# The third and fourth column block of the last gate's weights as two transfers, of 72 and of 56 rows

## Chip, cores and metric

The kernel runs on one core of one Trainium2 chip. The metric is the device time of one execution in microseconds (us), the median of several runs.

## The reference

The reference is one decode step of a transformer block with adaptive layer norm, for four sequences (B = 4) of one token, D = 512. Everything is in float32.

```
mod = silu(c) @ w_mod                 # c: 4 x 512, w_mod: 512 x 3072 -> six vectors of 512
sa, ca, ga, sb, cb, gb = mod
h = layernorm(x) * (1 + ca) + sa
x = x + ga * attention(h, k_cache, v_cache, wq, wo)   # 32 query heads, 8 key heads, last 2048 positions
h = layernorm(x) * (1 + cb) + sb
out = x + gb * ((silu(h @ w1) * (h @ w3)) @ w2)       # w1, w3: 512 x 1792, w2: 1792 x 512
```

The change concerns the weights of gb, the last of the six: gb = silu(c) @ w_mod[:, 2560:], a product of 4 x 512 with 512 x 512.

## The kernel before

The kernel is written for the engines directly: each engine has its own stream of instructions, and waits on semaphores by hand. The host lays every weight out so that a load is a plain copy of 128 rows, one for each SBUF partition. A load of rows of n columns is 128 x 4n bytes.

Three large buffers take the data: KV[0], KV[1] (64 KB in each of 128 partitions) and WP (32 KB). Attention runs over eight key heads, one after the other in KV[0] and KV[1]; WP holds the projections' weights for a pair of heads. After that the same buffers take the rest: KV[0] the modulation weights wm_in and the first feed-forward weights f1_in, KV[1] the rest of them (f2_in, two loads), the gate's weights gb_in, and then w2_in in six pieces of 4, 4, 2, 2, 1 and 1 blocks of 512 columns (W2_CUTS).

All large loads but one (t1_in, and the four rows of x, on ACT's queue) are issued by SP, in the order of the code, by `load(dst, src, sem)` (L89), which adds 16 to a semaphore once the transfer has landed. Before a buffer is filled anew, SP waits for the matmuls that read it. For KV[1]'s last contents that is L120, `S.wait_ge(o_done, G)`: the attention's last product. Behind it SP issues nine loads: f2_in twice, gb_in, w2_in six times (L121 to L125). Then it waits for the end to store the output.

gb_in holds w_mod's last 512 columns with 512 input rows laid out as four column blocks of 512 for each partition: partition p holds in block k the 512 weights of input row 128k + p. In KV[1] they lie in columns 6144 to 8191. Their one reader is the loop at L444 on TensorE: four matmuls, each with one block as its moving operand and 4 columns of sc (silu of c, transposed) as its weights. The results go to four groups of rows of the PSUM bank bM; ScalarE copies them to gb_sb (L448), and a later set of matmuls adds the four groups and turns them to the output's layout (L464).

The order of TensorE's work at the end: up and gate products from f1_in and f2_in, transposes of them (L437), `T.wait_ge(dgb, 16)` and gb's four matmuls, then for each piece of w2 a wait for its landing (L453) and its matmuls; between the pieces the sum of gb (after the first) and that of the first eight blocks of w2 (after the third). After the last piece come two operations of VectorE (L478, L480) and the store.

Of the kernel before, what the change touches and what calls it, by code (L numbers as in the profile page):

```python
# [43 lines left out]
def block_kernel(nc, x_in, t0_in, t1_in, kv_in, w_in, wm_in, f1_in, f2_in, gb_in, w2_in, out):  # L44
    T, v, s, gp, S = nc.tensor, nc.vector, nc.scalar, nc.gpsimd, nc.sync

    def sems(names):
        return [nc.alloc_semaphore(n) for n in names.split()]

    def sb(name, cols, rows=P):  # L50
        return nc.alloc_sbuf_tensor(name, (rows, cols), F32).ap()
# [8 lines left out]
    dx, dt0, dt1, dkv, dk, dva, dvb, dwo, dm, df1, df2a, df2b, dgb = sems("dx dt0 dt1 dkv dk dva dvb dwo dm df1 df2a df2b dgb")  # L60
# [5 lines left out]
    KV = [sb("KV0", 16384), sb("KV1", 16384)]  # L66
# [21 lines left out]
    def load(dst, src, sem):  # L88
        S.dma_start(dst, src).then_inc(sem, 16)  # L89
# [30 lines left out]
    S.wait_ge(o_done, G)  # L120
    load(KV[1][:, :3072], f2_in[:, :3072], df2a)  # L121
    load(KV[1][:, 3072:6144], f2_in[:, 3072:], df2b)
    load(KV[1][:, 6144:8192], gb_in, dgb)
    for a, b, sem in zip(W2_CUTS[:-1], W2_CUTS[1:], dw):
        load(KV[1][:, 8192 + a * 512 : 8192 + b * 512], w2_in[:, a * 512 : b * 512], sem)  # L125

# [313 lines left out]
    t_hid = V.op(v.tensor_mul(view(hidT)[:, :, :3], view(sT)[:, :, :3], view(bS)[:, :, :3, :B]))  # L440


    T.wait_ge(dgb, 16)
    for k in range(4):  # L444
        ins = mm(bM[32 * k : 32 * k + B, :], sc[:, k * B : (k + 1) * B], KV[1][:, 6144 + 512 * k : 6144 + 512 * (k + 1)])
    ins.then_inc(pe, 1)
# [85 lines left out]
```

## Time and profile before

| | |
|---|---|
| median of 3 runs | 242.96 us (242.74 to 242.99) |
| the profiled execution | 243.09 us, span 241.7 us |
| busy: PE, PEld, DVE, ACT, POOL | 137.8, 38.0, 38.6, 25.1, 1.7 us |
| granted TensorE clock, mean | 0.843 |
| bytes moved | 101.34 MB, 419 GB/s over the span |
| gb_in: bytes, issue to landing | 1024 KB, 22.8 us |

PE is TensorE's matmuls, PEld its weight loads, DVE is VectorE, ACT ScalarE, POOL GpSimd, SP the engine that issues the loads; PEq and SPq are the sequencers of PE and SP. The span runs from the first to the last instruction, and times in the trace count from its start. The 16 DMA engines of the core share each large transfer. A row "A <-B" names what is written and what is read; in the chain of work that ended last, each row has its start, its length and what ran then.

### The profile page before, as it was taken

The page shows a single profiled execution, that of the slowest core. Times are in us where ns is not written, and L with a number is a line of the kernel's source. Part 1 is how long each engine was busy: PE and PEld are TensorE (multiplying, and loading weights), DVE is VectorE, ACT ScalarE, POOL GpSimd, SP SyncE. Part 2 cuts the span into 40 slices and gives each one's busy share as a digit, 9 for nine tenths or more (in the row PEclk, how much of TensorE's full clock was granted, in tenths as well). Part 3 has the DMA queues.
Part 4 walks back from the last instruction along what each step waited for, and adds up shares of the span by engine and source line. Part 5 has one row for each costly group of instructions (what it writes and reads, how often), then busy time and mean ns, then how long its engine had stood idle before and what let it go on. Part 6 is the DMA issues. An engine that isn't in the chain of part 4 may idle for free. (4 is left out here: it accounts for less than half of the span.)

```text
span 241.7 us, 2238 instructions
## 1 busy us (share of the span) xinstructions
PE 137.8 (57%) x940; PEld 38.0 (16%) x940; DVE 38.6 (16%) x126; ACT 25.1 (10%) x54; POOL 1.7 (1%) x14
## 2 busy tenths in 40 slices
PE   3004677726771478267713782877137869656964
PEld 0000122201220013112200130121001312111211
DVE  3003203202200022022000220130002222133112
ACT  2002002100010011010100110011002100133110
POOL 2000000000000000000000000000000000000000
PEclk9999959968798579887985898679758997995999
DMA  7998989899989898999898989998989999999993
GB/s 266 440 511 358 510 361 499 369 423 439 504 369 499 369 499 370 423 428 504 369 499 369 499 369 423 434 510 369 499 347 445 442 396 445 449 431 394 413 415 116
DMA packets 4045, 101.34 MB, mean 419 GB/s; under 512 B 452, under 2 KB 580, under 8 KB 1096
## 3 DMA queue, kind: packets, MB, share of 16 engines
q1 hardware_dynamic: 3888, 99.17, 95.7%
q10 hardware_dynamic: 152, 2.11, 2.1%
q8 instruction: 3, 0.05, 0.1%
q14 instruction: 2, 0.02, 0.0%
HBM read 101.20 MB, written 0.07 MB: 419 GB/s over the span
## 5 line engine op out<-in xcount | busy, mean ns | idle before, releaser
L266 PE MATMUL bS<-KV,Z 128*16 128x512 f32 x256 | 42.7, 828 | 39.2 <-PEq L269 39.2
L266 PE MATMUL bO<-KV,pT 128*16 128x512 f32 x256 | 32.5, 652 | 0.5
L266 PEld LDWEIGHTS bS<-KV,Z 128*16 128x16 f32 x256 | 9.3, 123 | 67.1 <-issue 67.1
L222 DVE TENSOR_REDUCE MX<-bS 128x1 f32<-128x512 f32 x8 | 5.5, 692 | 80.4 <-PE bS L266 80.4
L266 PE MATMUL bM<-KV,sc 128*4 128x512 f32 x24 | 6.9, 801 | 16.6 <-DVE sc L188 16.6
L230 ACT ACTIVATE p_sb<-bS,NB 128x512 f32<-128x512 f32 x8 | 5.5, 687 | 101.2 <-DVE NB L228 101.2
L287 PE MATMUL bP<-ident,p_sb 128*128 128x128 f32 x32 | 5.6, 303 | 16.6 <-PEq L269 16.6
L266 PE MATMUL bA<-WP,oT 128*4 128x512 f32 x64 | 11.1, 773 | 4.3 <-PEq L269 4.3
L266 PEld LDWEIGHTS bO<-KV,pT 128*16 128x16 f32 x256 | 8.2, 107 | 23.9 <-issue 23.9
L251 ACT ACTIVATE o_sb<-bO,LB 128x512 f32<-128x512 f32 x8 | 5.5, 687 | 48.8 <-PE bO L266 48.8
L266 PE MATMUL bQ<-WP,hT 128*4 128x512 f32 x64 | 9.2, 647 | 0.6 <-DVE hT L197 0.6
L287 PE MATMUL bX<-ident,o_sb 128*128 128x128 f32 x32 | 5.0, 280 | 7.2 <-PEq L269 7.2
L254 DVE TENSOR_REDUCE oT<-bX 128x16 f32<-128x64 f32 x8 | 1.8, 224 | 43.6 <-PE bX L287 43.6
L287 PEld LDWEIGHTS bP<-ident,p_sb 128*128 128x128 f32 x32 | 3.6, 148 | 24.0 <-issue 24.0
L287 PE MATMUL bT<-ident,q_sb 128*128 128x128 f32 x32 | 5.5, 298 | 3.2 <-PEq L269 3.2
L201 ACT ACTIVATE q_sb<-bQ 128x512 f32<-128x512 f32 x8 | 4.7, 593 | 13.3 <-PE bQ L266 13.3
L287 PEld LDWEIGHTS bX<-ident,o_sb 128*128 128x128 f32 x32 | 3.4, 141 | 14.3 <-issue 14.3
L235 DVE COPY pT<-bP 128x256 f32<-128x256 f32 x8 | 3.4, 424 | 13.5 <-PE bP L287 13.5
L266 PE MATMUL bQ<-KV,h2T 128*4 128x512 f32 x32 | 5.3, 816 | 0.3 <-DVE h2T L398 0.3
L287 PEld LDWEIGHTS bT<-ident,q_sb 128*128 128x128 f32 x32 | 3.6, 150 | 8.0 <-issue 7.7
L266 PEld LDWEIGHTS bM<-KV,sc 128*4 128x4 f32 x24 | 1.0, 104 | 22.4 <-DVE sc L188 18.2
L266 PE MATMUL bX<-KV,sc 128*4 128x512 f32 x24 | 4.2, 592 | 0.0
(100 smaller groups left out, 65.2 us busy)
## 6 DMA issues: line engine op xcount, KB each, us to landing
WP<-w_in SPq DMA_DIRECT2D x3, 4096.0 KB, 22.0
KV<-kv_in SPq DMA_DIRECT2D x1, 4096.0 KB, 24.3
KV<-f_in SPq DMA_DIRECT2D x1, 4096.0 KB, 28.0
KV<-kv_in SPq DMA_DIRECT2D x1, 3072.0 KB, 31.1
KV<-wm_in SPq DMA_DIRECT2D x1, 3072.0 KB, 18.4
KV<-f_in SPq DMA_DIRECT2D x2, 1536.0 KB, 19.2
KV<-t_in SPq DMA_DIRECT2D x1, 2056.0 KB, 12.2
WP<-t_in ACTq DMA_DIRECT2D x1, 2048.0 KB, 12.4
```

What stands on the lines that cost most here:

```text
L201: A.op(s.mul(q_sb, bQ, DH**-0.5), q_ok)
L222: t = V.op(v.reduce_max(MX[:, 0:1], bS, axis=AX.X))
L230: A.op(s.activation(p_sb, bS, AF.Exp, bias=NB[:, 0:1], accum_out=SM[:, 0:1]), p_ok)
L235: v.tensor_copy(pT.rearrange("p (t b c r) -> p c b t r", t=NT, b=B, c=4), bP.rearrange("p (c b i) -> p c b i", c=4, b=B)[:, :, :, :16].rea ...
L251: A.op(s.mul(o_sb, bO, LB[:, 0:1]), o_ok)
L254: V.op(v.tensor_reduce(oT.rearrange("p (r b) -> p r b", r=R), diag, axis=AX.X, op=ALU.add), ot_ok)
L266: return T.matmul(o, lhsT, rhs, start=start, stop=stop, skip_group_check=True)
L287: ins = T.transpose(dst[:, c * P : (c + 1) * P], src[:, c * P : (c + 1) * P], ident)
```

## The change

gb_in comes as three transfers in place of one. The first has columns 0 to 1023 of all 128 rows, the first two blocks, 4 KB for each row. The second has the other two blocks for rows 0 to 71, the third for rows 72 to 127. All three add to the same semaphore, dgb, and TensorE waits for 48 instead of 16. The bytes, their places and their order in the queue, behind f2_in and ahead of w2_in, stay as they were.

```diff
@@ -120,7 +120,9 @@
     S.wait_ge(o_done, G)
     load(KV[1][:, :3072], f2_in[:, :3072], df2a)
     load(KV[1][:, 3072:6144], f2_in[:, 3072:], df2b)
-    load(KV[1][:, 6144:8192], gb_in, dgb)
+    load(KV[1][:, 6144:7168], gb_in[:, :1024], dgb)
+    for rows in (slice(0, 72), slice(72, 128)):
+        load(KV[1][rows, 7168:8192], gb_in[rows, 1024:], dgb)
     for a, b, sem in zip(W2_CUTS[:-1], W2_CUTS[1:], dw):
         load(KV[1][:, 8192 + a * 512 : 8192 + b * 512], w2_in[:, a * 512 : b * 512], sem)
@@ -440,7 +442,7 @@
-    T.wait_ge(dgb, 16)
+    T.wait_ge(dgb, 48)
     for k in range(4):
         ins = mm(bM[32 * k : 32 * k + B, :], sc[:, k * B : (k + 1) * B], KV[1][:, 6144 + 512 * k : 6144 + 512 * (k + 1)])
     ins.then_inc(pe, 1)
```

## The prediction

> **What bounds the kernel now.** I read the page's head and its slices of time, then the chain that ended last, the end of the timeline, and last the DMA engines' share in short windows of the end. The profiled execution took 243.09 us, its span 241.7; the median of the runs is 242.96, 0.13 us less, so a difference worked out on the trace is put on the median as it is. About 0.2%, 0.49 us, is what a measurement of this kernel can tell from no change.
>
> ```profile
> span 241.7 us, 2238 instructions
> DMA  7998989899989898999898989998989999999993
> DMA packets 4045, 101.34 MB, mean 419 GB/s; under 512 B 452, under 2 KB 580, under 8 KB 1096
> q1 hardware_dynamic: 3888, 99.17, 95.7%
> q10 hardware_dynamic: 152, 2.11, 2.1%
> DMA 12%; PE 3%; SPq 1%; DVE 0%; issue 0%
> KV<-gb_in SPq DMA_DIRECT2D x1, 1024.0 KB, 22.8
> ...
> 209.62 0.04 issue
> 209.67 0.43 SPq L89
> 210.10 0.04 issue
> 210.14 28.79 DMA KV<-w_in
> 238.93 0.04 issue
> 238.97 0.45 PE bX L266 x8
> 239.42 0.02 issue
> 239.44 0.30 DVE yt L478
> ```
>
> The 16 DMA engines are busy in nearly every slice, and the chain ends with the last piece of w2: issued by 210.14, landed at 238.93. From there to the end stand 2.7 us that nothing here touches. So the kernel ends when the slowest of the 16 engines has written its part of the last piece. Sixteen engines at 419 GB/s give 26.2 GB/s each: 4 KB in 0.156 us, 8 KB in 0.313 us.
>
> The packet counts tell how a transfer is dealt out. SP's queue has 27 transfers of 128 rows, and 3888 = 27 x (128 + 16): a packet for each row and one closing write for each engine. ACT's queue has one of 128 rows and x's four rows: 152 = (128 + 16) + (4 + 4). So four rows ran on four engines, 128 rows on sixteen.
>
> The next view is the end in windows: after the times, PE, PEld, DVE, ACT and POOL, the clock, the DMA engines' share and GB/s.
>
> ```profile
> 110.00:120.00 10.00, 7.53 (x52) 1.93 (x56) 1.18 (x6) 0.69 (x1) 0.00 (x0) 0.83 0.97 419
> ...
> 228.40:230.20 1.80, 1.79 (x12) 0.20 (x7) 1.13 (x4) 0.22 (x1) 0.00 (x0) 1.00 0.99 414
> 230.40:232.60 2.20, 1.52 (x12) 0.47 (x12) 0.74 (x2) 0.02 (x1) 0.00 (x0) 1.00 1.03 428
> 232.80:235.00 2.20, 1.23 (x16) 0.29 (x16) 0.00 (x0) 0.63 (x2) 0.00 (x0) 1.00 0.98 397
> ...
> 236.60:237.00 0.40, 0.40 (x16) 0.17 (x8) 0.37 (x1) 0.00 (x0) 0.00 (x0) 1.00 1.01 348
> 237.00:237.40 0.40, 0.40 (x12) 0.11 (x8) 0.00 (x0) 0.00 (x0) 0.00 (x0) 1.00 0.33 123
> 237.40:237.80 0.40, 0.11 (x8) 0.09 (x8) 0.00 (x0) 0.00 (x0) 0.00 (x0) 1.00 0.20 77
> 237.80:238.20 0.40, 0.40 (x16) 0.23 (x13) 0.00 (x0) 0.00 (x0) 0.00 (x0) 1.00 0.13 51
> 238.20:238.60 0.40, 0.37 (x16) 0.11 (x8) 0.00 (x0) 0.00 (x0) 0.00 (x0) 1.00 0.06 20
> 238.60:239.00 0.40, 0.19 (x12) 0.03 (x8) 0.00 (x0) 0.00 (x0) 0.00 (x0) 1.00 0.00 0
> ```
>
> Share times 16 is the number of engines still at work: 16 until 237.0, then 5.3, 3.2, 2.1, 1.0 in steps of 0.4 us, and none after 238.6. So about twelve engines end near 237.1, and four late ones near 237.5, 237.9, 238.2 and 238.5. The last is 1.4 us behind the twelve. The view doesn't number the engines.
>
> **The change, part by part.**
>
> Bytes for each engine. Now gb_in is 128 rows of 8 KB, eight rows or 64 KB an engine. Then 128 half rows of 4 KB come first, eight or 32 KB an engine. The 72 and the 56 rows that follow don't divide by 16. The packet counts fit "as many engines as divide the rows, at most 16", and by that 72 rows run on 12 engines with six rows each, and 56 on 14 with four each. Twelve engines then carry 8 + 6 + 4 = 18 rows of 4 KB, 72 KB, 8 KB more than now: 0.31 us. Two carry 48 KB, 16 KB less: -0.63 us. Two carry 32 KB, 32 KB less: -1.25 us. Shorter rows also cost: between the windows 230.4 to 232.6 (rows of 8 KB) and 232.8 to 235.0 (8 and 4 KB) the rate falls from 428 to 397 GB/s, so at most 8% of the 2.4 us that 64 KB take, 0.2 us, and at least nothing; I take 0.1. The twelve are 0.4 us later, two 0.5 earlier, two 1.2 earlier. If 72 rows ran on 16 engines after all, with four or five rows each, every engine would be within 4 KB, 0.16 us, of now. [...]
>
> Where the rows go. Every large transfer now spreads over 128 partitions, so at any time sixteen engines write to all of them. The trace can't tell whether 26.2 GB/s is the limit of an engine or of the eight partitions that it writes. The new ones go to partitions 0 to 71 and then 72 to 127, one half after the other, by 12 and 14 engines. The price has two ends. If the limit is the engine's, nothing is added to the sum above. If it is that of eight partitions, the first half takes at most 8 x 26.2 = 210 GB/s. 64 of the 72 rows go there, 256 KB, in 1.25 us, where six rows an engine would need 0.94. The 56 rows then all go to the other half, 224 KB in 1.07 us, where four rows an engine would need 0.62. Together 2.3 us instead of the 1.25 that the second 4 KB of all rows take now: an engine that carries both is 1.1 us later. A late engine fares worse. When it writes its ten rows, the early ones are at w2 already, and w2 goes to all partitions; with half of the rate its ten rows take 3.1 instead of 1.25 us, 1.9 later.
>
> The nearest rows are 419 GB/s in the window from 110 to 120 us, where the rows are 16 KB and longer, and 414 to 428 where they are 8 KB, all partitions in use. A limit that stays the same over such different rows doesn't come from the engines' work on each row, which leaves the width of the path between engine and partitions; of that path one end is as likely as the other to be the narrow one, and if both are equally wide, the partitions' end decides as soon as two engines meet there. So I take the crowding as the likelier, with both ends kept. [...] No row of this trace shows a large transfer to half of the partitions.
>
> Issues. SP issues two more transfers ahead of w2's six, 0.43 + 0.04 us each, so w2's are issued 0.94 us later. That costs nothing while the engines' queues are full. gb_in takes 22.8 us from issue to landing, nearly all of it behind earlier transfers, and this backlog covers the 0.94; without it the end would move by that much. SP has nothing else to do until the output.
>
> The wait. PE now waits for three landings of gb_in instead of one. Behind that wait on PE stand gb's matmuls and all of w2's; ACT waits for their result.
>
> ```profile
> 207.29 0.43 SPq L89 DMA_DIRECT2D KV<-gb_in  x1
> ...
> 230.99 0.55 PE L437 MATMUL bS<-ident,u_sb 96*128 96x96 f32 x4 [0.80 <-DVE u_sb L434]
> 231.47 1.04 PE L266 MATMUL bM<-KV,sc 128*4 128x512 f32 x8
> 232.58 0.59 ACT L448 COPY gb_sb<-bM 128x512 f32<-128x512 f32 x1 [3.95 <-PE bM L266]
> 232.77 1.04 PE L266 MATMUL bO<-KV,hidT 128*4 128x512 f32 x8 [0.26 <-DMA KV<-w_in]
> 235.16 1.04 PE L266 MATMUL bO<-KV,hidT 128*4 128x512 f32 x8 [1.14 <-DMA KV<-w_in]
> 237.71 1.05 PE L266 MATMUL bX<-KV,hidT 128*4 128x128 f32 x24 [0.29 <-DMA KV<-w_in]
> ```
>
> PE starts them at 231.47 without a wait. gb_in was issued at 207.29 and took 22.8 us, so it landed at 230.1, 1.4 us before. A delay up to 1.4 us is hidden there. With 1.9 us PE would start 0.5 later and finish at 233.0, where w2's first piece, later by as much, keeps it waiting until about 234.4 anyway. PE waits for w2 in each of the later rows, so it follows the DMA to the end, and what the last landing moves, the end moves.
>
> The sum with crowding. The twelve go from 237.1 to 238.2, below the 238.5 of now. A late engine that is one of the twelve decides: the third, 238.2 + 1.9 = 240.1, is 1.6 us after 238.5; the second, 237.9 + 1.9, 1.3; the last itself, 1.9. I take the middle, 1.6: 242.96 + 1.6 = 244.5 us.
>
> **The rivals.**
>
> Balance pays (faster). No crowding, and the four late engines are the four that are relieved. Then the late ones end at 238.5 - 1.2 = 237.3, the twelve at 237.1 + 0.4 = 237.5, and the end comes 1.0 us earlier, with 0.1 left for the spread of the twelve 0.9: 242.1. The amounts speak for it: 1.2 and 0.5 us is about what the late ones are behind by. Against it: nothing ties the late ones to the last four; it decides only if every late engine is among them. If just one that ends at 238.2 is not, it ends at 238.6 and the gain is gone.
>
> Balance that misses (no change). No crowding, and one or more of the late engines are among the twelve: the second late one gives 237.9 + 0.4 = 238.3, 0.2 us gained; the third 0.1 lost; the last 0.4 lost. So 242.8 to 243.4, within 0.2%. For it: four of sixteen engines are late, and only four are relieved. Against it: only the crowding. The same holds when 72 rows run on all 16 engines, at 0.16 us either way.
>
> Crowding with the late engines relieved. Then the twelve end last, at 238.2 and up to 0.6 later where two share a place with w2: 0.3 earlier to 0.3 later, no change that can be told.
>
> **How the numbers follow.** Crowding with a late engine among the twelve: 0.60, 244.5, its own range 243.9 to 245.9 (from 0.9 to 2.9: a late engine that meets two others at a place has a third of the rate for part of its rows, 1.0 more). Balance that misses and crowding with the late ones relieved: 0.28 together, 242.7 to 243.4. Balance pays: 0.12, 242.1. Slower is the first, same the second, faster the third. The range from 242.6 to 245.9 leaves out the third and the far end of the first.
>
> **What would show it.** With 12 and 14 engines SP's queue has 3888 + (72 + 12) + (56 + 14) = 4042 packets; 4048 would mean 16 for both. With crowding, the GB/s of the windows from 228 to 232 fall below the 414 to 428 of now, and w2's waits on PE grow; the number of engines at work past the bulk's end falls off over 2 us or more. Without crowding the windows keep their rates and only the last 1.5 us change. PE with an idle time before gb's matmuls would show that the cover of 1.4 us is gone. The prediction is wrong if an engine, and not the place written, sets the 26.2 GB/s.

## The result and the profile after

| | before | changed |
|---|---|---|
| median | 242.96 us (242.74 to 243.19, 5 runs) | 245.67 us (244.79 to 246.12, 5 runs) |
| ratio, 95% interval | | 1.0108 (1.0091 to 1.0126) |
| profiled execution, span | 243.09, 241.7 us | 244.79, 243.5 us |

The change makes the kernel 2.7 us slower. The profiled execution was the fastest of the changed kernel's five and shows 1.7 to 1.8 us of it, where those of e2, e6 and e11 below are the slowest of theirs, 1.6, 0.5 and 1.1 us above the median, and overstate the loss. The other 0.9 us of the change lie between runs, and no profile here shows them.

The page of the changed kernel, its DMA lines:

```profile
DMA packets 4199, 101.34 MB, mean 416 GB/s; under 512 B 478, under 2 KB 606, under 8 KB 1378
q1 hardware_dynamic: 4042, 99.17, 95.8%
```

The same bytes, in 4042 packets. That is the number for 72 rows on 12 engines and 56 rows on 14. The changed kernel in windows (columns as in the prediction; the last two are the DMA engines' share and GB/s; its line L268 is L266 of the kernel before):

```profile
224.00:226.00 2.00, 2.00 (x14) 0.30 (x8) 0.00 (x0) 0.00 (x0) 0.00 (x0) 0.52 0.94 393
226.00:228.00 2.00, 2.00 (x20) 0.38 (x12) 0.00 (x0) 0.59 (x1) 0.00 (x0) 1.00 1.04 313
228.00:230.00 2.00, 2.00 (x19) 0.72 (x16) 0.64 (x2) 0.22 (x1) 0.00 (x0) 1.00 1.06 231
230.00:232.00 2.00, 1.20 (x10) 0.35 (x4) 1.18 (x4) 0.00 (x0) 0.00 (x0) 1.00 0.99 291
232.00:234.00 2.00, 1.25 (x11) 0.13 (x9) 0.20 (x1) 0.59 (x1) 0.00 (x0) 1.00 1.01 422
```

From 226 to 232 us, while the parts of gb_in and then the first rows of w2 arrive, the engines are as busy as ever (shares of about 1) and move 313, 231 and 291 GB/s. After that the rate is 422 again. From 228 to 230 us that is a share of 1.06 at 231 GB/s, where the kernel before has 1.04 at 434: the engines were not idle, their transfers took longer. Over 226 to 234 us the kernel before and the changed one have:

```profile
226.00:234.00 8.00, 6.68 (x56) 1.73 (x50) 2.02 (x6) 1.21 (x3) 0.00 (x0) 1.00 1.00 416
```

```profile
226.00:234.00 8.00, 6.45 (x48) 1.58 (x40) 2.02 (x6) 1.40 (x3) 0.00 (x0) 1.00 1.02 314
```

102 GB/s less over 8 us are 0.82 MB, which at 419 GB/s take 1.9 us: so all that the trace shows of the loss is here. It lies on two kinds of rows. Between 227.0 and 231.4 us, 129 rows of 4 KB (the parts have 128) took 0.29 us each in the median, where others take 0.16; spread over 16 engines the excess is 1.1 us. And 77 of the 256 rows of 8 KB of w2's first two pieces, which go to all 128 partitions as before, took 0.52 instead of 0.31 us, another 1.0 us. The end of the changed kernel, first the windows, then the chain:

```profile
238.40:238.80 0.40, 0.40 (x16) 0.17 (x8) 0.36 (x1) 0.00 (x0) 0.00 (x0) 1.00 0.90 348
238.80:239.20 0.40, 0.40 (x12) 0.11 (x8) 0.00 (x0) 0.00 (x0) 0.00 (x0) 1.00 0.80 307
239.20:239.60 0.40, 0.12 (x7) 0.10 (x8) 0.00 (x0) 0.00 (x0) 0.00 (x0) 1.00 0.28 108
239.60:240.00 0.40, 0.40 (x16) 0.22 (x11) 0.00 (x0) 0.00 (x0) 0.00 (x0) 1.00 0.16 61
240.00:240.40 0.40, 0.39 (x14) 0.11 (x8) 0.00 (x0) 0.00 (x0) 0.00 (x0) 1.00 0.04 15
```

```profile
219.18 0.04 issue
219.22 21.50 DMA KV<-w_in
240.72 0.04 issue
240.76 0.45 PE bX L268 x8
```

The bulk of the engines stops near 239.2 instead of 237.1, the late ones near 240.3 instead of 238.5, and the last piece of w2 lands at 240.72 instead of 238.93, 1.79 us later. TensorE follows:

```profile
232.24 0.11 PEld L268 LDWEIGHTS bM<-KV,sc 128*4 128x4 f32 x8 [0.22 <-DMA KV<-gb_in]
232.24 1.04 PE L268 MATMUL bM<-KV,sc 128*4 128x512 f32 x8
...
234.56 1.04 PE L268 MATMUL bO<-KV,hidT 128*4 128x512 f32 x8 [1.28 <-DMA KV<-w_in]
```

The weight load ahead of gb's matmuls (PEld) now waits 0.22 us for gb_in, but w2's first piece keeps TensorE idle for 1.28 us after them, so this wait costs nothing by itself.

### The profile page after: what moved, and what is told of

Its sections match the earlier page's. It is cut to its first block, busy times and chain, and to the rows that moved or that the text cites. A ratio compares the mean times of both kernels' runs of the same rounds, so it can differ in the third digit from the quotient of the medians.

```text
span 243.5 us, 2240 instructions
## 1 busy us (share of the span) xinstructions
PE 131.9 (54%) x940; PEld 36.9 (15%) x940; DVE 38.6 (16%) x126; ACT 25.1 (10%) x54; POOL 1.7 (1%) x14
## 3 DMA queue, kind: packets, MB, share of 16 engines
q1 hardware_dynamic: 4042, 99.17, 95.8%
## 5 line engine op out<-in xcount | busy, mean ns | idle before, releaser
L268 PE MATMUL bS<-KV,Z 128*16 128x512 f32 x256 | 41.1, 800 | 46.7 <-PEq L271 46.7
L268 PE MATMUL bO<-KV,pT 128*16 128x512 f32 x256 | 29.7, 604 | 0.5
L268 PEld LDWEIGHTS bS<-KV,Z 128*16 128x16 f32 x256 | 9.0, 119 | 73.1 <-issue 73.1
L268 PE MATMUL bM<-KV,sc 128*4 128x512 f32 x24 | 6.4, 749 | 16.5 <-DVE sc L190 16.4
L268 PE MATMUL bA<-WP,oT 128*4 128x512 f32 x64 | 10.0, 703 | 2.4 <-PEq L271 2.4
L268 PEld LDWEIGHTS bO<-KV,pT 128*16 128x16 f32 x256 | 7.6, 100 | 20.7 <-issue 20.7
L268 PE MATMUL bQ<-WP,hT 128*4 128x512 f32 x64 | 8.4, 592 | 0.6 <-DVE hT L199 0.6
L268 PE MATMUL bQ<-KV,h2T 128*4 128x512 f32 x32 | 6.3, 961 | 0.9 <-DMA KV<-f_in 0.9
L289 PE MATMUL bT<-ident,q_sb 128*128 128x128 f32 x32 | 5.0, 280 | 3.2 <-PEq L271 3.2
L268 PEld LDWEIGHTS bM<-KV,sc 128*4 128x4 f32 x24 | 0.9, 100 | 21.8 <-DVE sc L190 18.0
L268 PE MATMUL bX<-KV,sc 128*4 128x512 f32 x24 | 3.6, 592 | 0.8 <-DMA KV<-wm_in 0.8
```

Of the source, the lines that this page charges most:

```text
L268: return T.matmul(o, lhsT, rhs, start=start, stop=stop, skip_group_check=True)
L289: ins = T.transpose(dst[:, c * P : (c + 1) * P], src[:, c * P : (c + 1) * P], ident)
```

## The experiments

Theory: crowding. Engines that deal out 72 or 56 rows write to the same group of partitions at a time and hold each other up. Rivals: the cost of more and shorter transfers (overhead), engines with more bytes than others (uneven engines), a limit on the side that is read. Each kernel is the kernel before with another load of gb_in and the wait to match. Differences are between medians, against the kernel before in the same series. e5, e6, e7, e9, e10, e11 and e12 leave a part of gb_in out, so they tell what a transfer costs and are no versions to use.

| run | gb_in comes as | difference, us | ratio, 95% interval |
|---|---|---|---|
| e1 | 128 rows three times | +0.26 | 1.0009 (1.0000 to 1.0018) |
| e2 | 128 rows; 0-63; 64-127 | +2.71 | 1.0117 (1.0099 to 1.0136) |
| e3 | 0-71; 72-127, all blocks | +5.01 | 1.0217 (1.0203 to 1.0230) |
| e4 | 128 rows; 0-111; 112-127 | +2.15 | 1.0085 (1.0072 to 1.0098) |
| e5 | 128 rows, first half only | -1.32 | 0.9947 (0.9933 to 0.9960) |
| e6 | as e5, and 0-63 | +0.95 | 1.0037 (1.0024 to 1.0051) |
| e7 | as e5, and 32-95 | -0.56 | 0.9979 (0.9970 to 0.9988) |
| e8 | 128 rows; 32-95; 0-31; 96-127 | +1.49 | 1.0061 (1.0047 to 1.0075) |
| e9 | as e5, and 32-87 | -0.66 | 0.9972 (0.9961 to 0.9983) |
| e10 | as e5, and 32-71 | -1.13 | 0.9960 (0.9946 to 0.9974) |
| e11 | 0-63 alone, all blocks | +2.26 | 1.0086 (1.0072 to 1.0100) |
| e12 | 32-95 alone, all blocks | -1.17 | 0.9948 (0.9935 to 0.9961) |

**e1, three transfers without parts.**

```diff
+    load(KV[1][:, 6144:7168], gb_in[:, :1024], dgb)
+    load(KV[1][:, 7168:7680], gb_in[:, 1024:1536], dgb)
+    load(KV[1][:, 7680:8192], gb_in[:, 1536:], dgb)
```

> gb_in as three transfers, but all of 128 rows: two blocks, one block, one block; the wait for 48 stays. Crowding (two or more engines write to the same group of partitions at a time): nothing is crowded, so 0 to 0.3 us over before, from the shorter rows alone. Rival, overhead (more transfers, shorter rows, two more issues, three closing writes): as many transfers as in the changed kernel and rows as short or shorter, so the whole 1.7 to 2.7 us. Rival, uneven engines: 0, every engine has 64 KB.

Measured: +0.26 us, with 413 GB/s where the changed kernel has 314:

```profile
226.00:234.00 8.00, 7.20 (x60) 1.80 (x56) 2.02 (x6) 1.40 (x3) 0.00 (x0) 1.00 1.02 413
```

Two more transfers, two more landings to wait for and rows as short as 2 KB cost a tenth of the change. Overhead of this kind is out as its cause. A cost of any transfer of fewer than 128 rows isn't, before e7.

**e2, equal halves.**

```diff
+    load(KV[1][:, 6144:7168], gb_in[:, :1024], dgb)
+    for rows in (slice(0, 64), slice(64, 128)):
+        load(KV[1][rows, 7168:8192], gb_in[rows, 1024:], dgb)
```

> As the changed kernel, but the third and fourth block come as rows 0 to 63 and 64 to 127, four rows for each of 16 engines: every engine carries 64 KB as before. Crowding: each half takes 1.25 us at 8 x 26.2 GB/s instead of 0.62, so +1.2 us, up to 2.1 where late engines meet the others' w2; the rate falls to 300 GB/s or less for some 3 us as in the changed kernel. Uneven engines: nothing is uneven, so within 0.2 us of before. Overhead: as the changed kernel, +1.7 to 2.7.

Measured: +2.71 us, as much as the changed kernel's +2.71, with no uneven engine (4048 packets, 16 engines for each transfer):

```profile
q1 hardware_dynamic: 4048, 99.17, 95.3%
```

```profile
226.00:234.00 8.00, 5.81 (x44) 1.56 (x36) 2.02 (x6) 0.81 (x2) 0.00 (x0) 1.00 1.02 263
```

So the uneven share of 12 and 14 engines isn't needed for the cost. The size is above what crowding was expected to cost, 1.2 to 2.1.

**e3, all four blocks in 72 and 56 rows.**

```diff
+    for rows in (slice(0, 72), slice(72, 128)):
+        load(KV[1][rows, 6144:8192], gb_in[rows], dgb)
```

> All four blocks as two transfers, 72 and 56 rows of 8 KB, no transfer of 128 rows: the bytes that come in parts are doubled. Crowding: the cost goes with those bytes, twice that of the changed kernel, +3.4 to 5 us. Uneven engines: twelve engines have 80 KB, 16 KB more, so an engine that is late ends 0.6 us later and the kernel with it: +0.6. Overhead: one transfer less and longer rows than in the changed kernel, so less than its 1.7, about +1.

Measured: +5.01 us, 1.85 times the change for twice the bytes in parts, and one transfer fewer. The cost goes roughly with the bytes.

**e4, 112 and 16 rows.**

```diff
+    load(KV[1][:, 6144:7168], gb_in[:, :1024], dgb)
+    for rows in (slice(0, 112), slice(112, 128)):
+        load(KV[1][rows, 7168:8192], gb_in[rows, 1024:], dgb)
```

> Third and fourth block as rows 0 to 111 (seven for each of 16 engines) and 112 to 127 (one each): every engine carries 64 KB. Crowding by halves, as the prediction has it: 64 of the 112 rows are in the lower half and 48 in the upper, so little is lost there, at most 0.1, and the last 16 rows lie in a narrow strip, a quarter of a half, 64 KB at a few times 26.2 GB/s: +0.3 to 0.7 us. Crowding by the way rows are dealt to engines (any transfer that isn't of 128 rows gives an engine other partitions than its own, so engines meet whatever the span): +1.4 to 2.4. Uneven engines: within 0.2. Overhead: as the changed kernel, +1.7 to 2.7.

Measured: +2.15 us.

```profile
226.00:234.00 8.00, 6.78 (x52) 1.68 (x44) 2.02 (x6) 1.04 (x3) 0.00 (x0) 1.00 1.02 313
```

Here 112 of 128 partitions are in one transfer, 64 of them in one half and 48 in the other, and every engine has 64 KB by the deal that the packet counts fit (seven rows and one); the cost is four fifths of the change all the same. "One half after the other", as the prediction put it, is not what makes the crowd. That speaks for the way rows are dealt to engines, an inference: no view shows the deal.

**e5, the price of the bytes.** Third and fourth block left out:

```diff
+    load(KV[1][:, 6144:7168], gb_in[:, :1024], dgb)
```

> Only the first two blocks of gb_in come, as 128 rows of 4 KB; the third and fourth block are left out (gb's sum is then made with old data in their place). It prices the bytes: 32 KB less for each engine at 26.2 GB/s. All theories: -1.2 us.

Measured: -1.32 us for 32 KB an engine; 1.25 at 26.2 GB/s.

**e6 and e7, the same shape at other partitions.** e5 and one more transfer, which is all that differs between the two. How 64 rows are dealt to the 16 engines, four in a row to each or one by one, no view shows.

```diff
+    load(KV[1][0:64, 7168:8192], gb_in[0:64, 1024:], dgb)      # e6
+    load(KV[1][32:96, 7168:8192], gb_in[32:96, 1024:], dgb)    # e7
```

> As the run without the third and fourth block, plus rows 0 to 63 of these two blocks, four rows for each of 16 engines; rows 64 to 127 of them are left out. Crowding: the half takes 1.25 us or more instead of 0.62, so not the -0.6 that its bytes give against before but 0 to +0.7. A limit on the reading side, or a cost of any transfer of fewer rows: the same as the run with rows 32 to 95. No such limit: -0.6.

> As the run with rows 0 to 63, but the rows are 32 to 95: as many bytes, rows and engines, other partitions. [...] If 64 rows are dealt one by one, neighbours meet in either case: +0.1 to +0.7, like rows 0 to 63. Reading side or cost of the shape: equal to rows 0 to 63.

Measured: e6 +0.95 (above the 0 to +0.7 of crowding), e7 -0.56 us, 1.51 us between them. e6, then e7:

```profile
226.00:234.00 8.00, 6.57 (x52) 1.58 (x40) 2.02 (x6) 1.37 (x3) 0.00 (x0) 1.00 1.02 329
```

```profile
226.00:234.00 8.00, 7.20 (x56) 1.79 (x48) 2.02 (x6) 1.32 (x3) 0.00 (x0) 0.98 1.01 415
```

The bytes, the number of rows and of packets (so of engines) are the same, and the rate is 329 or 415 GB/s. This is the pair that decides: a transfer of 64 rows costs little but its bytes at 32 to 95 (-0.56 us against before, where 16 KB less for each engine at 26.2 GB/s are -0.63) and 1.51 us more at 0 to 63. The author's reading is that at 32 to 95 each engine writes partitions that no other writes at the time, and that at 0 to 63 two share them; that is not shown. The rows read differ too; they lie in one array at the same spacing, but no run read the same rows into other partitions, so that the reading side has no part in it is argued, not shown.

In e6 the slow rate also outlasts the rows of the part. From 230.4 to 231.6 us both runs move rows of w2 alone, which go to all 128 partitions (the only packets under 8 KB are closing writes, under 512 B), e6 at 273 and e7 at 437 GB/s:

```profile
DMA packets 46, 0.33 MB, mean 273 GB/s; under 512 B 6, under 2 KB 6, under 8 KB 6
```

```profile
DMA packets 68, 0.52 MB, mean 437 GB/s; under 512 B 4, under 2 KB 4, under 8 KB 4
```

**e8, everything, with the middle first.**

```diff
+    load(KV[1][:, 6144:7168], gb_in[:, :1024], dgb)
+    for rows in (slice(32, 96), slice(0, 32), slice(96, 128)):
+        load(KV[1][rows, 7168:8192], gb_in[rows, 1024:], dgb)
```

> All data again: first two blocks as 128 rows, the other two as rows 32 to 95, then 0 to 31, then 96 to 127. Crowding with rows dealt four in a row: the middle costs nothing, each outer quarter runs two engines to a group of partitions, +0.6 to 1.3 us over before, about half of the +2.7 of the run with rows 0 to 63 and 64 to 127. Dealt one by one: no gain from the middle, +1.2 to 2.7. Overhead: one transfer more than in the changed kernel, so at least its cost.

Measured: +1.49 us, a little over the upper end, 55% of e2's cost with one transfer more and the same bytes, about what it would be if half of the rows crowd. It is still no gain: nothing tried here beats the kernel before with all data loaded. In the profiles of e8, e2 and e3 the granted TensorE clock is 0.5 for 6.8 us near the end, and TensorE, not the last landing, ends the chain. This adds little: the last row of w2 lies 3.35, 3.35 and 3.50 us ahead of the end there, 3.15 in the kernel before.

**e9 and e10, uneven engines without a crowd.** As e7, with fewer rows, and so without a crowd if rows 32 to 95 have none. By the deal that the packet counts fit, 56 rows run on 14 engines and 40 rows on ten, four rows each, and the other six engines have none of the 40.

```diff
+    load(KV[1][32:88, 7168:8192], gb_in[32:88, 1024:], dgb)    # e9
+    load(KV[1][32:72, 7168:8192], gb_in[32:72, 1024:], dgb)    # e10
```

> [...] Uneven engines without crowding: two engines have 16 KB less than in the run with rows 32 to 95, the other fourteen the same. If a late engine that ends last is one of these two, the end moves by up to 0.2 us (then the second late one decides), to -0.8 against before; if not, -0.6 as with rows 32 to 95. Overhead or partial shapes: no difference either.

> [...] No crowding. If the last engine is one of the ten, -0.6 us as with rows 32 to 95; if the last one is of the other six, -0.8 (the second late one decides), and -1.2 only if all late ones are of the six. [...]

Measured: -0.66 and -1.13 us, against -0.56 for e7. The windows at the end of e7, e9 and e10:

```profile
237.20:237.60 0.40, 0.30 (x12) 0.29 (x16) 0.00 (x0) 0.00 (x0) 0.00 (x0) 1.00 0.13 51
237.60:238.00 0.40, 0.40 (x16) 0.13 (x12) 0.00 (x0) 0.00 (x0) 0.00 (x0) 1.00 0.09 36
```

```profile
237.20:237.60 0.40, 0.35 (x16) 0.32 (x16) 0.00 (x0) 0.00 (x0) 0.00 (x0) 1.00 0.14 51
237.60:238.00 0.40, 0.40 (x20) 0.11 (x8) 0.00 (x0) 0.00 (x0) 0.00 (x0) 1.00 0.11 41
```

```profile
237.20:237.60 0.40, 0.40 (x12) 0.11 (x8) 0.00 (x0) 0.00 (x0) 0.00 (x0) 1.00 0.06 20
237.60:238.00 0.40, 0.18 (x8) 0.09 (x8) 0.00 (x0) 0.00 (x0) 0.00 (x0) 1.00 0.00 0
```

By the share times 16, two engines still work from 237.2 to 237.6 with rows 32 to 95 (share 0.13) and with 32 to 87 (0.14); with rows 32 to 71 it is one (0.06), and after 237.6 none. If the same engines are late in each run and the ten are all among the fourteen, neither of which a view shows, the last ones are not the two that e9 relieves, and they are among the six that e10 relieves: the four in between. Two of e10's six executions took 242.65 and 242.66 us, 0.5 us under the kernel before as in e7, so it doesn't hold for every execution. If 72, 56 and 40 rows all start from the same engine, the author's estimate and not shown, the change gives two of these four more and two less.

**e11 and e12, the dose.**

```diff
+    load(KV[1][0:64, 6144:8192], gb_in[0:64], dgb)      # e11
+    load(KV[1][32:96, 6144:8192], gb_in[32:96], dgb)    # e12
```

> gb_in as one transfer of rows 0 to 63, all four blocks, rows of 8 KB; rows 64 to 127 are left out. Twice the bytes per row of the run with rows 0 to 63 of two blocks, in one transfer. If the 1.5 us that rows 0 to 63 cost over rows 32 to 95 go with the bytes (two engines at one group of partitions get together about 16 instead of 26 GB/s), it ends 3.0 us after its counterpart with rows 32 to 95, +1.8 us over before. If they were a cost of each crowded transfer, 1.5 us after it, +0.3. If two engines shared the full 26.2 GB/s of a group fairly, 1.25 us after it, 0.

> As the run before it with rows 32 to 95 of all four blocks; the other 64 rows are left out. [...]

Measured: +2.26 and -1.17 us, 3.43 between them, against 1.51 for half of the bytes; +2.26 is above the 1.8 of the reading by bytes, and -1.17 is near the -1.25 that 32 KB less for each engine are at 26.2 GB/s. e11, then e12:

```profile
226.00:234.00 8.00, 6.15 (x48) 1.68 (x44) 1.98 (x6) 0.81 (x2) 0.00 (x0) 1.00 0.99 248
```

```profile
226.00:234.00 8.00, 6.90 (x60) 1.77 (x53) 2.02 (x6) 1.62 (x4) 0.00 (x0) 1.00 1.00 414
```

The crowd cost roughly by the byte here (2.3 times for twice the bytes, 3.43 against 1.51 us), not by the transfer.

## Why the prediction was right, and where its sizes were off

The direction and the cause of the loss held: the engines stay busy and the bytes slow down while parts of the rows are written. The size and the path to the end were off: it forecast +1.6 us, and the median says +2.7.

- Deal: 72 rows on 12 engines, 56 on 14. The 4042 packets are the number given. No run shows which engines these are: that the twelve are all among the fourteen, on which the sums with twelve, two and two engines rest, was an estimate.
- Crowding. The prediction let two engines share 26.2 GB/s, an estimate, so that the bulk of the engines is 1.1, a late one 1.9 us later. For the parts themselves this came out: their rows cost 1.1 us, spread over 16 engines. What it put at nothing for the bulk, in the sum that gives 244.5, is w2's rows behind, another 1.0 us; only a late engine, and the twelve in a rival (0.6), were to meet w2. In the changed kernel's profile the bulk moved by 2.1 us (237.1 to 239.2) and the late ones by 1.8 (238.5 to 240.3): the whole field moved, and no late engine had to be among the twelve for the end to move. That +1.6, the delay of a late engine among the twelve, is near the profile's +1.8 is luck.
- Its reason for the crowd, one half of the partitions after the other, fell with e4, where one transfer fills 64 partitions of one half and 48 of the other and crowds all the same. e7 has 32 of each half, so it fits the reason too. What counts, by e4, e6, e7 and e8 together, is which partitions a transfer covers; that it is a matter of whether each engine gets partitions of its own is inferred, and no view shows the deal.
- Uneven engines: the +0.4 us for the twelve engines with more bytes can't be told in any run; e2 without it is as slow as the change.
- The range ends at 245.9, the far end of crowding's own range, so it doesn't leave that end out, as the prediction says.
- "A late engine among the twelve": open. e9 and e10 put the last ones among four engines, if the ten are among the fourteen; that the change gives two of them more and two less is an estimate.
- "Balance pays" needed every late engine to be among the four relieved. The crowd hid whether it is so: the late ones are still 1.1 us behind the bulk in the changed kernel, 1.4 before.
- Shorter rows and issues: e1 has as many issues as the change and more short rows, and costs 0.26 us. The issues of gb_in were to take 0.94 us more, hidden. They do:

```profile
205.65 1.37 SPq L89 DMA_DIRECT2D KV<-gb_in  x3
```

1.37 against the 0.43 us of one, and the last issue of w2 is 21.5 us ahead of its landing.

- The cover of gb's matmuls, 1.4 us, was used up (0.22 us of wait), and w2's first piece hid that, as written.

## What to carry to other kernels

A load that is split by rows cost more than its bytes here, even with the same share for every engine: 2.71 us for e2's halves. Keep to transfers of all 128 rows, and split by columns, which cost 0.26 us (e1), a tenth as much. Where a profile has DMA engines busy and their GB/s down, as here a share of 1.06 at 231 GB/s, look at which partitions are written at the same time before counting bytes for each engine. A comparison of two kernels that differ only in the range of partitions (e6 and e7, 1.51 us apart) tells this apart from the cost of the bytes, of the number of transfers and of their shape.

## What was not expected of the hardware

The rows behind a crowd were slow too: w2's ran at 273 GB/s behind rows 0 to 63 and at 437 behind rows 32 to 95. Rows 0 to 63 take 1.51 us longer than rows 32 to 95 for 256 KB, which spread out need 0.62. Charged to these bytes alone that is 2.1 us, 123 GB/s, and for 512 KB 1.25 + 3.43 = 4.7 us, 112 GB/s, where fair sharing at 8 x 26.2 would be 210. But e6's trace shows another split. 62 of its rows of 4 KB (the part has 64) took longer than usual, 0.32 us in the median instead of 0.16: that is what fair sharing by two would give, 205 GB/s for 16 engines. The loss beyond it lies on w2's rows of 8 KB: 107 of 256 took 0.46 us in the median, where e7 has 0.31. Spread over 16 engines, the crowded rows cost 0.6 us and w2's 1.2.

Why w2's rows stay slow isn't settled; engines out of step, some at w2 where others still write the parts, would be one reason, a guess that no view shows. That 64 rows are dealt four in a row to each engine is the author's reading of e6 and e7, which e8's +1.49 us, over the upper end of 1.3, fits by half; no run shows it.
